# Attention and expert layers on one core: all expert matmuls as two halves side by side on 64x128 tiles

## The chip, the core and the metric

The kernel runs on one core of a Trainium2 chip. A core has five engines that run their own queues in order and meet at semaphores: TensorE (PE) for matmuls, VectorE (DVE), ScalarE (ACT), GpSimd (POOL) and SyncE (SP), which issues most DMAs. The metric is the device time of one execution in microseconds (us); lower is better.

## What is computed

Eight batches of 448 tokens, 12 heads of 64, all float32. First attention with capped scores, then a layer of one expert, in which each batch sends its 128 best tokens through two matrices:

```python
scores = cap * np.tanh(scale * np.matmul(q, k.transpose(0, 1, 3, 2)) / cap)
attn = np.exp(scores - max)
out = np.matmul(attn / (attn.sum(-1) + 1e-09), v)      # -> x, (8, 448, 768)
...
scores = np.einsum('bsd,d->bs', x, w_gate)
for b in range(B):
    top_idx = np.argpartition(-scores[b], capacity)[:capacity]   # 128 of 448
    xe = x[b, top_idx]
    ye = np.maximum(xe @ w1, 0.0) @ w2                  # 768 -> 1024 -> 768
    g = 1.0 / (1.0 + np.exp(-scores[b, top_idx]))
    out[b, top_idx] = x[b, top_idx] + g[:, None] * ye
```

## The kernel before

The order of all instructions on all engines is made before the program is built, by a planner inside the kernel (`Sim`, `Task`, `Front`): each step is a `Task` with an engine, an assumed duration, events that it depends on, and slots of rings (buffers) that it takes and releases. The planner plays the steps through and writes them out in that order; on the chip the engines keep this order and wait at semaphores. A wrong duration in it makes no error, only a wait.

**Attention** is done by a `Double`: four heads of one batch, 24 in all. A Double has four units of 128 keys, the last of 64; two such tails make one score unit, so there are 84 score units and 96 value units. A score unit (`scores_mm`) fills `K.S4`, four PSUM banks, of which there is one set. ACT turns it into one of four buffers `K.p` with a tanh, which frees `K.S4`, and an exponential in place (`score_task`). `values_mm` multiplies `p` with `v` (28 matmuls, each of two passes) and accumulates a Double's units in two PSUM banks, which DVE divides and evacuates (`output_proc`).

**Tile forms.** PE can split its 128 rows and columns. In the rows of the trace `64*128 64x448` means a part of 64 rows by 128 columns with a moving operand of 64 partitions by 448 elements. Scores of the first four Doubles and of all tails are float32 on 64x64 parts; the other scores are three products of split operands (`kh`, `kl`, `qh`, `ql`: a float32r part and the rest) on two 64x128 parts that work side by side, into different banks. Values use 128x64 parts (64x64 for tails). Everything of the expert uses the whole 128x128 array (`FULL`).

**The expert.** When a batch's three Doubles are out, `select_proc` sums the gate scores (`total`), joins the two halves of the last column with a matmul (`join`), turns the four columns into a row on all partitions with four transposes (`turn`), and copies the row out of PSUM. DVE compares every score with the row (`greater`, `ties`), which gives ranks, a one-hot matrix and, by `pick` on PE, the token numbers and scores. POOL gathers the rows of the 128 tokens from the output in DRAM. `expert_proc` transposes them (`split_tasks`), splits them into high and low, and multiplies by `w1` in two halves of 512 columns, 18 matmuls each; then relu, transposes, `w2` in two halves of 384 columns, 24 matmuls each; `combine` on DVE adds the result, and POOL scatters the rows back. Two PSUM banks (`T`, `H`) serve all of this until attention ends, when the six banks of scores and values are added.

**The order on PE** is chosen in `Front.policy` between the next score unit (Q), the next value unit (V) and expert steps (F). Costs of a change of form are `SWITCH` and `AFTER`; `LEAST`, `MOST` and `due` set how much expert work is put between, `second_value` lets a value unit wait for another. SP's queue holds the loads of q, k, v and the stores of the output, in the order planned.

Of the kernel before, what the change touches and what calls it, by code (L numbers as in the profile page):

```python
# [16 lines left out]
P = 128  # L17
HD = 64
# [6 lines left out]
FAR = 1e6  # L25


QUARTER, TALL, WIDTH, FULL = range(4)
SWITCH, AFTER = 100, 45
MARGIN = 150  # L30
RESERVE = 50000
LEAST, MOST = 1500, 2200
# [5 lines left out]
PS, PG, PH = 1.1, 1.1, 1.2  # L38
IDLE = 2000
# [181 lines left out]
def allocate(tc, K):  # L221
# [17 lines left out]
    K.twice = t("twice", [P, P])  # L239
# [3 lines left out]
    K.before = t("before", [P, NCH * P], BF16)  # L243
    K.gst = [t(f"gst{i}", [P, 4]) for i in range(2)]
    K.part = [t(f"part{i}", [P, K.NG, NCH]) for i in range(2)]
    K.jk, K.jt = t("jk", [P, S], BF16), t("jt", [P, S], BF16)
# [8 lines left out]
    K.p = ring("p", 4, [P, 4, S])  # L255
# [8 lines left out]
    K.row = ring("row", 1, [P, S])  # L264
# [15 lines left out]
    K.acc = [Ring([bank(tc, K.stack, f"V{i}", [P, 512])]) for i in range(2)]  # L280
    K.banks = Ring([bank(tc, K.stack, c, [P, 512]) for c in "TH"])


def lent(K, nm, dt):
    return K.work.tile([P, 2, K.S], dt, tag="x" + nm, name=nm + "lent")

# [11 lines left out]
def split_scores(tc, K):  # L298
    K.score_stack.close()
    K.score_stack = ExitStack()  # L300
    return [bank(tc, K.score_stack, c, [P, 512]) for c in "ABCD"]


def load_flag(tc, K, cap):
# [3 lines left out]
    warm = K.banks.slots[1].obj  # L308
# [9 lines left out]
def load_consts(tc, K):  # L318
# [75 lines left out]
class Double:  # L394

    def __init__(self, K, d):
# [5 lines left out]
        if d % 2:  # L402
            self.units = self.units[-1:] + self.units[:-1]
# [4 lines left out]
        self.accs = None  # L408
# [20 lines left out]
    def split(self, tc, K):  # L429
        nc = tc.nc  # L430
        for nm in "kq":
# [3 lines left out]
            def high(t, nm=nm, raw=raw):  # L435
# [7 lines left out]
                refs=[K.NCH - 1] * 2, prio=1.2, kind="high")  # L443
# [41 lines left out]
def values_mm(tc, K, D, c):  # L485
    p, v = D.P[c], D.at("v")
    full = K.NCH - 1
    for i in range(K.NS):
        for r in range(2):
            for g in range(2):  # L490
# [3 lines left out]
                tc.nc.tensor.matmul(D.accs[r].obj[HALF[g], i * WIDE:(i + 1) * WIDE],  # L494
# [15 lines left out]
def output_proc(tc, K, D):  # L510
# [9 lines left out]
    def evac(t, r):  # L520
# [3 lines left out]
        blocks = D.accs[r].obj[:, :K.NS * WIDE].rearrange("p (i w) -> p i w", w=WIDE)  # L524
# [51 lines left out]
def select_proc(tc, K, b):  # L576
# [5 lines left out]

    def total(t):
# [6 lines left out]
    t = yield Task("DVE", 380, total, deps=K.scored[b], take=[K.score], refs=[4 + 2 * NCH],  # L590
# [4 lines left out]
    last = NCH - 1  # L595

    def join(t):
        nc.tensor.matmul(t.slots[0].obj[:, S:S + 1], lhsT=K.twice, rhs=score[:, last:],
                         start=True, stop=True)
# [3 lines left out]
    bank, rs = j.slots  # L603
    row = rs.obj
    j = yield Task("DVE", 130, lambda t: nc.vector.tensor_copy(
        score[:, last:], bank.obj[:, S:S + 1]), deps=[j], reads=[sc], prio=1, kind="joined")

    def turn(t):
        for c in range(NCH):
            nc.tensor.transpose(bank.obj[:, c * P:(c + 1) * P],  # L610
                                score[:, c:c + 1].to_broadcast([P, P]), K.ident)
# [8 lines left out]
    for c in range(NCH):  # L620
# [5 lines left out]
        def ties(t, c=c):  # L626
            m = rows_of(c)
            n = min(P * (c + 1), S)
            at = P * (NCH - 1 - c)
            nc.vector.scalar_tensor_tensor(out=K.jt[:m, :n], in0=row[:m, :n],  # L630
                                           scalar=score[:m, c:c + 1],
                                           in1=K.before[:m, at:at + n],
# [16 lines left out]
    for n in range(chunks):  # L649
# [709 lines left out]
```

## Time and profile before

| | us |
|---|---|
| runs shown | 462.6, 464.11, 465.36 |
| median | 464.11 |
| profiled execution | 464.68 |
| its span, first to last instruction | 463.0 |
| PE busy | 446.5 |
| ACT busy | 311.1 |
| DVE busy | 264.6 |

The durations below come from the profiled execution. A row of the timeline has a start, the time to the end of the last of its instructions, and how many there are; matmuls overlap, so the step from one start to the next tells what one costs the queue. Floats of 32 bits that are no float32r run as two instructions each. In brackets stands an idle time ahead of the row and what released it. The mean clock granted to TensorE was 0.994 of full speed.

### The profile page before, as it was taken

What the parts mean: (1) busy time and instruction counts of PE and PEld (TensorE: products, weight loads), DVE (VectorE), ACT (ScalarE), POOL (GpSimd) and SP (SyncE); (2) the same over time, 40 slices, a digit from 0 to 9 for tenths busy, and PEclk for the clock granted to TensorE, in tenths of its full rate; (3) what the DMA queues carried; (4) which work ended last, traced back from release to release, by engine and by line L of the source; (5) the groups of instructions that cost most, each with busy time, mean ns of one, the idle gap of its engine ahead of it and who ended that gap; (6) DMA issues with size and microseconds to landing.
All of it is one profiled execution on the core that took longest, in us unless ns stands there. A gap on an engine that the chain in (4) does not pass through costs nothing.

```text
span 463.0 us, 16297 instructions
## 1 busy us (share of the span) xinstructions
PE 446.5 (96%) x7358; PEld 363.3 (78%) x7358; DVE 264.6 (57%) x784; ACT 311.1 (67%) x202; POOL 22.1 (5%) x53
## 2 busy tenths in 40 slices
PE   6999998999999999999999999999999998999994
PEld 3665676878878878788788788887787896988984
DVE  1087789977439735379368386674289336342321
ACT  4899999987886868795978896877869741010010
POOL 2000000100000001000001000001000001001000
PEclk9999999999999999999999999999999999999998
DMA  7977475355252253271272432434422102011001
GB/s 233 376 228 240 141 266 197 95 180 166 81 180 64 82 193 120 81 237 48 61 254 78 151 132 83 149 95 150 164 87 75 42 23 89 30 40 55 15 35 39
DMA packets 31886, 58.52 MB, mean 126 GB/s; under 512 B 9920, under 2 KB 19904, under 8 KB 31808
## 3 DMA queue, kind: packets, MB, share of 16 engines
q1 hardware_dynamic: 30528, 51.10, 34.0%
q0 software_dynamic: 1280, 6.29, 4.2%
q8 instruction: 59, 0.97, 0.9%
q14 instruction: 19, 0.16, 0.1%
HBM read 43.23 MB, written 14.16 MB: 124 GB/s over the span
## 4 chain that ended last, share of the span: by engine, by line
PE 79%; issue 10%; ACT 5%; DMA 3%; DVE 2%; SPq 0%; POOL 0%; POOLq 0%; DVEq 0%; ACTq 0%
PE psV L494 27%; PE psS L471 16%; PE psS L481 8%; PE psH L771 6%; PE psT L771 4%; PE psH L808 3%; ACT p L923 3%; PE psT L808 3%; PE psD L808 2%; PE psC L771 2%; PE psV L808 2%; ACT p L930 2%; DMA out<-xe,idx 2%; PE psT L710 1%; PE psA L808 1%
## 5 line engine op out<-in xcount | busy, mean ns | idle before, releaser
L923 ACT ACTIVATE p<-psS,sc 128x1792 f32<-128x1792 f32 x84 | 147.5, 1756 | 61.7 <-PE psS L471 42.9
L494 PEld LDWEIGHTS psV<-v,p 128*64 128x64 f32 (+1 forms) x5152 | 139.3, 137 | 24.9 <-issue 15.5
L930 ACT ACTIVATE p<-p,capc 128x1792 f32<-128x1792 f32 x84 | 150.6, 1792 | 2.4
L494 PE MATMUL psV<-v,p 128*64 128x65 f32 (+1 forms) x5152 | 148.6, 223 | 1.8 <-DVE xt L531 1.2
L471 PE MATMUL psS<-qh,kh 64*128 64x448 f32 x240 | 50.3, 415 | 1.3 <-ACT p L923 1.1
L481 PE MATMUL psS<-q,k 64*64 64x448 f32 x328 | 37.4, 572 | 3.7 <-ACT p L923 3.4
L440 DVE CAST kh<-k 128x896 fp32r<-128x896 f32 x20 | 12.5, 625 | 41.1 <-DMA k<-in_k 34.4
L525 DVE RECIPROCAL rec<-psV 128x7 f32<-128x7 f32 x48 | 9.6, 200 | 41.4 <-PE psV L494 41.4
L471 PEld LDWEIGHTS psS<-qh,kh 64*128 64x128 f32 x240 | 22.6, 184 | 12.2 <-issue 5.2
L560 DVE CUSTOM_DVE_ANT_0 jk<-xn,wg 128x256 bf16<-128x256 f32 x72 | 30.3, 420 | 1.2
L526 DVE TENSOR_TENSOR xn<-psV,rec 128x384 f32<-128x384 f32 x48 | 26.8, 558 | 1.7
L481 PEld LDWEIGHTS psS<-q,k 64*64 64x64 f32 x328 | 11.0, 137 | 16.8 <-issue 10.6
L471 PE MATMUL psS<-qh,kl 64*128 64x448 f32 x120 | 22.1, 362 | 0.0
L471 PE MATMUL psS<-ql,kh 64*128 64x448 f32 x120 | 22.1, 362 | 0.0
L471 PE MATMUL psS<-qh,klent 64*128 64x448 f32 x120 | 22.0, 363 | 0.0
L471 PE MATMUL psS<-qlent,kh 64*128 64x448 f32 x120 | 22.0, 362 | 0.0
L623 DVE TENSOR_SCALAR_CACHE_REDUCE jk<-row,score 128x448 bf16<-128x448 f32 (+1 forms) x32 | 21.5, 672 | 0.2
L784 ACT ACTIVATE hs<-psH 128x512 f32<-128x512 f32 x8 | 4.7, 593 | 24.4 <-PE psH L771 24.4
L683 ACT ACTIVATE gt<-gt 128x1 f32<-128x1 f32 x8 | 1.6, 194 | 26.0 <-DVE gt L680 25.9
L630 DVE SCALAR_TENSOR_TENSOR jt<-row,score,before 128x128 bf16<-128x128 f32 (+3 forms) x32 | 16.9, 527 | 0.0
L460 POOL MEMSET v<- 128x14 f32 x23 | 3.0, 132 | 265.7 <-DMA v<-in_v 196.6
L852 POOL DMA_INDIRECT out<-xe,idx x8 | 8.2, 1021 | 142.5 <-DVE xe L824 122.4
(212 smaller groups left out, 623.5 us busy)
## 6 DMA issues: line engine op xcount, KB each, us to landing
v<-in_v SPq DMA_DIRECT2D x23, 455.0 KB, 3.4
q<-in_q SPq DMA_DIRECT2D x22, 448.0 KB, 4.8
k<-in_k SPq DMA_DIRECT2D x22, 448.0 KB, 6.2
out<-xn SPq DMA_DIRECT2D x24, 384.0 KB, 2.9
stage<-in_moe_w SPq DMA_DIRECT2D x4, 512.0 KB, 7.3
stage<-in_moe_w SPq DMA_DIRECT2D x5, 384.0 KB, 4.3
out<-xt SPq DMA_DIRECT2D x48, 32.0 KB, 2.7
hs<-in_moe_w SPq DMA_DIRECT2D x3, 384.0 KB, 5.7
```

The source lines that it names most:

```text
L440: nc.vector.tensor_copy(t.slots[0].obj, self.at(nm))
L471: tc.nc.tensor.matmul(K.S4[:, 2 * r + j, :K.S], lhsT=a[HALF[j], r, c * P:(c + 1) * P], rhs=b[HALF[j], r, :], start=(n == 0), stop=(n == 2))
L481: tc.nc.tensor.matmul(K.S4[HALF[half], n, :K.S], lhsT=k[HALF[j], r, at:at + HD], rhs=q[HALF[j], r, :], start=True, stop=True)
L494: tc.nc.tensor.matmul(D.accs[r].obj[HALF[g], i * WIDE:(i + 1) * WIDE], lhsT=p[rows, h, n * HD:(n + 1) * HD], rhs=v[rows, u, :], start=(c = ...
L526: nc.vector.tensor_tensor(slots[0].obj.rearrange("p c (r j d) -> p r j c d", r=2, j=2)[:, r], blocks[:, :2 * full, :K.D].rearrange("p (j c ...
L560: nc.vector.tensor_tensor_reduce(out=K.jk[:, :x.shape[1]], in0=x, in1=g, scale=1.0, scalar=0.0, op0=ALU.mult, op1=ALU.add, accum_out=part[ ...
L623: nc.vector.tensor_scalar(K.jk[:m], row[:m], score[:m, c:c + 1], None, op0=ALU.is_gt, op1=ALU.add, accum_out=rk.obj[:m, 0, c:c + 1])
L630: nc.vector.scalar_tensor_tensor(out=K.jt[:m, :n], in0=row[:m, :n], scalar=score[:m, c:c + 1], in1=K.before[:m, at:at + n], op0=ALU.is_equ ...
L771: nc.tensor.matmul(ph[:M], lhsT=(xh, xl)[part][:, i, :M], rhs=K.wts[r][:, i, fs], start=(n == 0), stop=(n == len(ops) - 1))
L808: nc.tensor.matmul(bank[0].obj[:M, :HH], lhsT=hp[0].obj[part][:, i, :M], rhs=K.wts[r][:, i, ds_], start=(start and n == 0), stop=(stop and ...
L923: nc.scalar.activation(slot.obj, K.S4[:, :, :K.S], AF.Tanh, scale=K.sc)
L930: nc.scalar.activation(slot.obj, slot.obj, AF.Exp, scale=K.cap)
```

## The change

Every expert matmul (`group`) becomes two: the upper and lower 64 rows of the contraction, side by side on 64x128 parts. In the first turn of a layer rows 0 to 63 write the bank of the left half of the columns and rows 64 to 127 that of the right half; in the second turn they change banks. Between the turns stands a drain of PE. Transposes (`split_tasks`), which now do all of a layer's blocks into one slot, and `pick` are cut in the same way, and what reads them joins two banks. PSUM slots are pairs of banks: one slot `T` for the expert in place of `T` and `H`, one for the accumulators.

The row of scores no longer passes PE: `put` stores the 128x4 scores in a line in DRAM, `get` loads the line onto all partitions, and DVE joins the last column (`sums`). The row has the tokens in another order and is 512 long, so the masks for ties change.

In the planner `FULL` goes, `SWITCH` and `AFTER` are 110 and 85 for 100 and 45, expert steps may stand directly beside scores of their form, and value units come in runs of up to four or to the end of a Double (`run_ready`). From Double 6 on the tails' score unit stands ahead of the even Double instead of the odd one, and the even Double's values begin with the tail. Relu may run on DVE.

```diff
-SWITCH, AFTER = 100, 45
+SWITCH, AFTER = 110, 85
...
+LATE = 3000
+RUN, SLACK = 4, 300
+SIDE = 6
+DRAIN = 100
...
-        if d % 2:
+        if d % 2 == (1 if d < SIDE else 0):
             self.units = self.units[-1:] + self.units[:-1]
...
-    K.acc = [Ring([bank(tc, K.stack, f"V{i}", [P, 512])]) for i in range(2)]
-    K.banks = Ring([bank(tc, K.stack, c, [P, 512]) for c in "TH"])
+    K.acc = Ring([bank(tc, K.stack, "V", [P, 2, 512])])
+    K.banks = Ring([bank(tc, K.stack, "T", [P, 2, 512])])
...
-    j = yield Task("PE", 250, join, deps=[t], take=[K.banks, K.row], refs=[1, 2 * NCH],
-                   reads=[sc], prio=(0, 3 * b), kind="join")
...
-    r = yield Task("PE", 400, turn, deps=[j], reads=[sc], prio=(0, 3 * b), kind="turnrow")
-    r = yield copy_task(tc, S, lambda _: row, lambda _: bank.obj[:, :S], deps=[r],
-                        reads=[bank], prio=1, kind="rowcopy")
...
+    def put(t):
+        nc.sync.dma_start(t.slots[0].obj.rearrange("o (p c) -> (o p) c", c=NCH), score)
+
+    def get(t):
+        nc.sync.dma_start(t.slots[0].obj, ln.obj.to_broadcast([P, NCH * P]))
+
+    def sums(t):
+        tail = places[:, :HD, last]
+        nc.vector.tensor_tensor(tail, tail, places[:, HD:, last], op=ALU.add)
+        nc.vector.memset(places[:, HD:, last], NEVER)
+        nc.vector.tensor_tensor_reduce(out=K.jk[:HD, :HD], in0=tail[:HD], in1=K.ident[:HD, :HD],
+                                       scale=1.0, scalar=0.0, op0=ALU.mult, op1=ALU.add,
+                                       accum_out=score[:HD, last:])
+
+    w = yield Task("SP", 700, put, deps=[t], take=[K.line], refs=[1], reads=[sc], lag=900, prio=0,
+                   kind="put")
+    ln = w.slots[0]
+    r = yield Task("SP", 700, get, deps=[w], take=[K.row], refs=[2 * NCH], reads=[ln], lag=900,
+                   prio=0, kind="get")
...
+    r = yield Task("DVE", 600, sums, deps=[(r, LATE)], reads=[sc], prio=1, kind="joined")
...
-                nc.tensor.matmul(t.slots[0].obj[:, :4], lhsT=sel.obj[:, c, :],
-                                 rhs=vals[:, :, c], start=(c == 0), stop=(c == NCH - 1))
+                for h, half in enumerate(HALF):
+                    nc.tensor.matmul(t.slots[0].obj[:, h, :4], lhsT=sel.obj[half, c, :],
+                                     rhs=vals[half, :, c], start=(c == 0), stop=(c == NCH - 1))
...
         for i in range(w):
-            nc.tensor.transpose(pt[:, i, :M], src[:M, (at + i) * P:(at + i + 1) * P],
-                                K.ident[:M, :M])
+            for h, half in enumerate(HALF):
+                nc.tensor.transpose(t.slots[0].obj[:, h, i * HD:(i + 1) * HD],
+                                    src()[half, i * P:(i + 1) * P], K.ident[half, half])
...
+def group(tc, K, kind, prio, pair, parts, wts, n, width, cost):
+    nc = tc.nc
+    ops = [(0, wts + "h", i) for i in range(n)] + [(0, wts + "l", i) for i in range(n)]
+    ops += [(1, wts + "h", i) for i in range(n)]
+    last = len(ops) - 1
...
+    for m in range(2 * len(ops)):
+        turn, at = divmod(m, len(ops))
+        part, r, i = ops[at]
...
+            if m == last + 1:
+                gap.append(nc.tensor.drain().ins)
...
+            for h in (0, 1) if m != last else (1, 0):
+                g = h ^ turn
+                ins = nc.tensor.matmul(bank.obj[:, g, :width],
+                                       lhsT=pair.obj[part][HALF[h], i, :],
+                                       rhs=K.wts[r][HALF[h], i, g * width:(g + 1) * width],
+                                       start=(m == 0), stop=(m == 2 * last + 1)).ins
...
+            if D.d >= SIDE and D.d % 2 == 0:
+                self.work.append([(D, full), (Ds[D.d + 1], full)])
...
-        if seg == "F":
-            order = "FQV" if self.left > 0 else "QVF"
-        elif f and not big and not self.backlog(t, IDLE):
-            order = "VFQ" if seg == "Q" and two else "FVQ" if seg == "Q" else "QFV"
...
+        run = self.run_ready(t)
+        if run:
             order = "VQF"
...
+            order = "QFV"
```

The order of instructions shows it in two places. First PE, where the first layer of the second batch's expert is multiplied. L471 is a score unit (six such rows make one), L771 an expert matmul into bank `psT` or `psH`, L494 values. Before, from a score unit on:

```order
L471 MATMUL psS<-qh_104,klent 128x448 x2
L771 MATMUL psT<-w1l,xh 128x512 x5
L771 MATMUL psT<-w1h,xl 128x512 x5
L471 MATMUL psS<-qh_103,kh_101 128x448 x2
...
L471 MATMUL psS<-qh_103,kl_105 128x448 x2
L494 MATMUL psV_129<-v_88,p_90 64x65 x2
...
L494 MATMUL psV_133<-v_88,p_91 64x65 x2
...
L771 MATMUL psT<-w1h,xl 128x512
L771 MATMUL psH<-w1h,xh 128x512 x6
```

After, the same layer (L484 scores, L778 expert halves, two to a pair, L507 values, 28 to a unit):

```order
L484 MATMUL psS<-qh_104,kl_106 128x448 x2
L778 MATMUL psT<-w1h,xh 128x512 x12
L778 MATMUL psT<-w1l,xh 128x512 x6
L484 MATMUL psS<-qh_104,kh_102 128x448 x2
...
L778 MATMUL psT<-w1h,xh 128x512 x10
L778 MATMUL psT<-w1l,xh 128x512 x10
L507 MATMUL psV<-v_90,plent 64x65 x28
L507 MATMUL psV<-v_90,p_91 64x65 x28
L507 MATMUL psV<-v_90,p_92 64x65 x28
L507 MATMUL psV<-v_90,p_93 64x65 x28
```

Scores and expert halves alternate in three score units, and four value units follow in one run, where two stood between two score units.

Second SP, at a batch's last output stores in the middle of the program (`xn`, `xt` are stored, `v`, `q`, `k` loaded). Before:

```order
L546 DMA out<-xn_95 384x1x256
L549 DMA out<-xt_98 64x2x64 x2
L415 DMA q_85<-in_q 128x896
L415 DMA k_87<-in_k 128x896
L415 DMA q_84<-in_q 128x896
```

After:

```order
L559 DMA out<-xn_95 384x1x256
L562 DMA out<-xt_99 64x2x64 x2
L611 DMA line_113<-score_116 128x4
L614 DMA row_110<-line_113 128x512
L428 DMA v_89<-in_v 128x910
```

The store of the scores and the load of the row stand between the output's stores and the next loads.

## Rows read from the trace of the kernel before

**Rows 1.** The page: PE's line of part 1, and part 4 by engine.
```profile
PE 446.5 (96%) x7358; PEld 363.3 (78%) x7358; DVE 264.6 (57%) x784; ACT 311.1 (67%) x202; POOL 22.1 (5%) x53
PE 79%; issue 10%; ACT 5%; DMA 3%; DVE 2%; SPq 0%; POOL 0%; POOLq 0%; DVEq 0%; ACTq 0%
```
**Rows 2.** Busy time of each engine in four stretches.
```profile
0.00:95.00 95.00, 86.93 (x1774) 61.62 (x1776) 64.78 (x175) 81.98 (x49) 4.46 (x22) 0.98 0.68 224
95.00:378.00 283.00, 282.48 (x5171) 232.62 (x5169) 168.69 (x526) 221.99 (x140) 9.81 (x23) 1.00 0.37 118
378.00:457.20 79.20, 77.05 (x425) 69.02 (x421) 30.94 (x84) 7.15 (x14) 6.84 (x7) 1.00 0.13 42
457.20:463.00 5.80, 0.00 (x0) 0.00 (x0) 0.23 (x1) 0.00 (x0) 0.97 (x1) 0.79 0.21 75
```
**Rows 3.** Timeline of PE: start us, us, instruction; scores, expert, scores.
```profile
177.21 0.48 PE L471 MATMUL psS<-qh,kh 64*128 64x448 f32 x2
177.52 0.37 PE L471 MATMUL psS<-qlent,kh 64*128 64x448 f32 x2
...
178.34 0.37 PE L471 MATMUL psS<-qh,klent 64*128 64x448 f32 x2
178.63 1.43 PE L771 MATMUL psT<-w1l,xh 128*128 128x512 f32 x5
...
181.16 0.47 PE L471 MATMUL psS<-qh,kh 64*128 64x448 f32 x2
```
**Rows 4.** Timeline of PE: one value unit, three in a row, one tail.
```profile
223.28 1.85 PE L494 MATMUL psV<-v,p 128*64 128x65 f32 x56
225.06 0.47 PE L471 MATMUL psS<-qh,kh 64*128 64x448 f32 x2
...
276.20 5.12 PE L494 MATMUL psV<-v,p 128*64 128x65 f32 x168
281.25 0.47 PE L471 MATMUL psS<-qh,kh 64*128 64x448 f32 x2
...
235.08 1.05 PE L494 MATMUL psV<-v,p 64*64 64x65 f32 x56
236.05 0.79 PE L808 MATMUL psT<-w2h,hh 128*128 128x384 f32 x3
```
**Rows 5.** Timeline of PE: expert matmuls undisturbed, w1 and w2.
```profile
438.99 1.56 PE L771 MATMUL psH<-w1h,xh 128*128 128x512 f32 x6
440.39 1.56 PE L771 MATMUL psH<-w1l,xh 128*128 128x512 f32 x6
...
453.14 0.86 PE L808 MATMUL psT<-w2l,hh 128*128 128x384 f32 x4
453.83 0.85 PE L808 MATMUL psT<-w2h,hl 128*128 128x384 f32 x4
```
**Rows 6.** Timeline of PE: joining and turning the row, and transposes of the expert.
```profile
383.26 0.36 PE L598 MATMUL psB<-score,twice 128*128 128x1 f32 x2
383.48 0.48 PE L771 MATMUL psH<-w1l,xh 128*128 128x512 f32 x1
...
386.13 0.65 PE L610 MATMUL psB<-ident,score 128*128 128x128 f32 x4 [1.70 <-DVE score L605]
386.54 0.72 PE L771 MATMUL psH<-w1h,xl 128*128 128x512 f32 x2
...
407.45 0.60 PE L710 MATMUL psV<-ident,hs 128*128 128x128 f32 x4
407.81 0.48 PE L771 MATMUL psC<-w1h,xh 128*128 128x512 f32 x1
408.12 1.10 PE L771 MATMUL psC<-w1l,xh 128*128 128x512 f32 x4
```
**Rows 7.** Timeline of PE's weight loads in a score unit.
```profile
177.52 0.19 PEld L471 LDWEIGHTS psS<-qh,klent 64*128 64x128 f32 x2
177.73 0.19 PEld L471 LDWEIGHTS psS<-qh,kh 64*128 64x128 f32 x2
```
**Rows 8.** Timeline of ACT, where it is never idle.
```profile
88.59 1.73 ACT L923 ACTIVATE p<-psS,sc 128x1792 f32<-128x1792 f32 x1
90.35 1.79 ACT L930 ACTIVATE p<-p,capc 128x1792 f32<-128x1792 f32 x1
...
95.80 1.76 ACT L923 ACTIVATE p<-psS,sc 128x1792 f32<-128x1792 f32 x1
```
**Rows 9.** DMA issues (KB each, us to landing), and what SP's queue waited for.
```profile
k<-in_k SPq DMA_DIRECT2D x22, 448.0 KB, 6.2
out<-xt SPq DMA_DIRECT2D x48, 32.0 KB, 2.7
xe<-out,idx POOLq DMA_INDIRECT x8, 3.9
SPq L415 <- PE psV L494: 132.9, 24, 10.8
```
**Rows 10.** Timeline from attention's end to the last batch's pick: PE, DVE, PE.
```profile
378.31 0.79 PE L808 MATMUL psT<-w2h,hh 128*128 128x384 f32 x3
...
382.41 0.16 DVE L587 TENSOR_TENSOR score<-score,part 128x4 f32<-128x4 f32 x1
385.59 0.16 DVE L678 TENSOR_SCALAR idx<-psA 128x1 int32<-128x1 f32 x1 [3.02 <-DMA out<-xe,idx]
...
386.82 0.62 DVE L505 COPY row<-psB 128x448 f32<-128x448 f32 x1 [0.19 <-PE psB L610]
...
394.19 0.86 DVE L661 TENSOR_SCALAR sel<-iota,rk 128x128 fp32r<-128x128 f32 x4
...
403.98 0.50 PE L670 MATMUL psD<-vals,sel 128*128 128x4 f32 x4
```
**Rows 11.** Timeline of the end.
```profile
456.81 0.62 DVE L824 SCALAR_TENSOR_TENSOR xe<-psA,gt,xe 128x384 f32<-128x384 f32 x1 [1.47 <-PE psA L808]
```

More of the change, by code (lines that the diff above doesn't have):

```diff
@@ L263, in allocate @@
         raw.free.append(raw.slots[-1])
-    K.row = ring("row", 1, [P, S])
+    K.row = ring("row", 1, [P, NCH * P])
+    lines = K.stack.enter_context(tc.tile_pool(name="lines", bufs=1, space=bass.MemoryType.DRAM))
+    K.line = Ring([lines.tile([1, NCH * P], F32, name=f"line{i}") for i in range(2)])
     K.sel = ring("sel", 1, [P, NCH, P], F32R)
@@ L581, in select_proc @@
     part = K.part[b % 2]
+    last = NCH - 1
     def total(t):
@@ L589, in select_proc @@
     chunks = -(-K.C // P)
-    t = yield Task("DVE", 380, total, deps=K.scored[b], take=[K.score], refs=[4 + 2 * NCH],
+    t = yield Task("DVE", 380, total, deps=K.scored[b], take=[K.score], refs=[3 + 2 * NCH],
                    prio=1, kind="total")
@@ L593, in select_proc @@
     score = sc.obj
[L595 to L599, printed above, removed]
-    j = yield Task("PE", 250, join, deps=[t], take=[K.banks, K.row], refs=[1, 2 * NCH],
-                   reads=[sc], prio=(0, 3 * b), kind="join")
-    bank, rs = j.slots
-    row = rs.obj
[L605 to L611, printed above, removed]
-    r = yield Task("PE", 400, turn, deps=[j], reads=[sc], prio=(0, 3 * b), kind="turnrow")
-    r = yield copy_task(tc, S, lambda _: row, lambda _: bank.obj[:, :S], deps=[r],
-                        reads=[bank], prio=1, kind="rowcopy")
+    def put(t):
[14 more added lines that the diff above has]
+                   prio=0, kind="get")
+    rs = r.slots[0]
+    row = rs.obj
+    places = row.rearrange("p (a c) -> p a c", c=NCH)
+    r = yield Task("DVE", 600, sums, deps=[(r, LATE)], reads=[sc], prio=1, kind="joined")
     r = [r]
@@ new lines, in turn @@
+            for h, half in enumerate(HALF):
+                nc.tensor.transpose(t.slots[0].obj[:, h, i * HD:(i + 1) * HD],
+                                    src()[half, i * P:(i + 1) * P], K.ident[half, half])
+    t = yield Task("PE", 111 * w, turn, deps=dep, take=[K.banks, take],
+                   refs=[2 * len(parts), 0], reads=reads, prio=prio, kind=kind)
+    bank, pair = t.slots
+    if take is K.xs and not isinstance(pair.obj, tuple):
+        pair.obj = (K.work.tile([P, K.ND, P], F32R, tag="xh", name="xh"), K.xl)
@@ new lines, in expert_proc @@
+    yield [t]
+    hp, parts = yield from split_tasks(tc, K, lambda: relus[0].obj, [t], K.hp, [relus[0]],
+                                       K.NF, (0, 3 * b + 2), "turnh")
+    hp.refs = 1
+    yield [K.weights["w2"]]
+    if not K.tail:
+        yield [p for pair in parts.values() for p in pair]
+    HH = K.DM // 2
+    bank, t = yield from group(tc, K, "w2", prio, hp, parts, "w2", K.NF, HH, 177)
+    ends = [sim.add(Task("DVE", 534, lambda _, g=g: nc.vector.scalar_tensor_tensor(
+        out=xe.obj[:, g * HH:(g + 1) * HH], in0=bank.obj[:, g, :HH], scalar=gt.obj,
+        in1=xe.obj[:, g * HH:(g + 1) * HH], op0=ALU.mult, op1=ALU.add), deps=[t, gate],
+        reads=[bank, gt], prio=1, kind="combine")) for g in range(2)]
```

366 lines of the change are left out of this document (150 added, 216 removed).

## The prediction

> **What bounds the kernel now.** I read the page first. TensorE (PE) is busy 446.5 of 463.0 us and the chain that ended last lies on it for 79% [rows 1]. The table of stretches says where the rest is: up to 95 us PE is busy 86.93 us and ScalarE (ACT) 81.98; from 95 to 378 us, while scores, values and expert work alternate, PE is busy 282.48 of 283.00; from there to 457.2 us it works off the experts that are left, 77.05 of 79.20; the last 5.8 us are the end of the last expert [rows 2]. So from 95 us on the time is what stands in PE's queue, laid end to end. "Busy" hides gaps in a pipelined engine, so I went to start times. A score unit on 64x128 tiles starts at 177.21, its pairs of matmuls follow each other every 0.205 us (177.52 to 178.34, four steps), and the expert's first matmul starts at 178.63: 1.42 us for six pairs that need 6 x 0.205 = 1.23 [rows 3]. The ten expert matmuls behind it take 178.63 to 181.16 = 2.53 us; where such matmuls run undisturbed six take 1.40 us (0.233 each), so ten need 2.33 [rows 3, 5]. Values on 128x64 tiles: one block of 28 takes 1.78 us, three in a row 5.05, so a block needs 1.635 and a run pays 0.145 once; on 64x64 tiles a block takes 0.97 [rows 4]. **Each run of one tile form thus pays about 0.19 (scores), 0.20 (expert), 0.15 us (values)**, half behind its last matmul and half before its second.
>
> **Runs of one form.** Counting runs in the two instruction orders gives 202 before (60 of 64x128, 53 of 128x64, 48 of 128x128, 41 of 64x64) and 133 after (45, 51, 1, 36): the expert's runs join those of the scores. 15 x 0.19 + 47 x 0.20 + 2 x 0.145 + 5 x 0.15 = **-13.3 us**.
>
> **The score row leaves PE.** Per batch the joining matmul (383.26 to 383.48, 0.22) and the four turning transposes (386.13 to 386.54, 0.41) go: 8 x 0.63 = **-5.1 us**; the wait of 1.70 us for the joined column, once, goes too, **-1.7** [rows 6].
>
> **Expert matmuls.** 672 whole ones become 672 pairs of halves. A score pair, two halves side by side, takes 0.205 us for 448 columns; whole matmuls take 0.233 for 512 and 0.69/4 = 0.173 for 384 [rows 3, 5], and between these 448 would be 0.203. So a pair costs a whole one: 0. The 112 transposes become pairs of half the width. Now one takes (0.67 - 0.233)/4 = 0.11 us [rows 6]. A pair may take half of that (-6 us in all), if only columns count, or twice (+12), if the two weight loads came one after the other. But a score pair's two loads end together, 0.19 us for both [rows 7], so I take 0 again, and likewise for the 32 picks.
>
> **Drains.** Each of 16 layers is cut once by a drain, where the halves change banks. The trace has no such instruction. The nearest row is a change of form, 0.20 us [rows 3]; less than nothing it can't be, since the queue only waits there; twice that is my upper end. 16 x 0.20 = **+3.2** (0 to 6.4).
>
> **ACT.** A unit occupies ACT for a tanh and an exponential, 88.59 to 95.80 us for two units, 3.6 us each where ACT is the limit [rows 8]. Where PE comes to the next scores sooner, it waits. I added up what stands in PE's order between one score unit and the next. Past the 24th unit, where expert work begins, six such periods in the old order are under 3.55 us and lack 1.4 us of 3.6 in all. In the new one there are 22, lacking 5.6, for two reasons: a run without changes is shorter for the same work (score, 18 halves: 1.23 + 2.10 plus one change), and with one PSUM slot for all expert steps there is none to lay between while a layer is emptied. **+4.2** (0, if the slack after long value runs absorbs it, to 7, if ACT's copies of 0.5 us fall there). The first 24 units stay ACT's: nothing gained there.
>
> **The row through DRAM.** SP gets a store and a broadcast load per batch; the load waits for the store's landing, and loads of v, q, k queue behind it. They have cover: SP already spends 132.9 us in 24 waits for PE to release v [rows 9]. The chain from total to pick grows. A landing takes 2.7 us (small store) to 6.2 (k) [rows 9], so two take 5.4 to 12.4. For the last batch the total is ready at 382.6, 4.3 us after attention's end (378.31), and from the row's copy at 386.82 to the one-hot at 394.19 to 395.05 are 8.2 us; its pick ran only at 403.98 [rows 10]. After the change some 22 us of PE work (expert matmuls and transposes, by the steps above) stand between the last values and that pick. The chain needs 4.3 + 5.4 to 12.4 + about 9 = 19 to 26 us. VectorE (DVE) also waited 3.02 us for an earlier scatter to release the index [rows 10], and the transposes of the next tokens follow the pick by about 5 us of PE work, where a gather takes 3.9 to land [rows 9]. In the tail I put **+1.5** (0 to 4). Elsewhere the experts run a batch behind the attention, and wider comparisons (512 for 448) lie on a DVE that is busy 168.69 of 283 us [rows 2].
>
> **The end.** The two halves of the last layer finish together, so a second combine of 0.62 us [rows 11] follows the first: **+0.6**. The scatter after it is the same.
>
> **Sum.** -13.3 - 5.1 - 1.7 + 3.2 + 4.2 + 1.5 + 0.6 = -10.6 us. The profiled execution took 464.68 us (span 463.0), inside the 462.6 to 465.36 of the runs with median 464.11; 464.68 - 10.6 = 454.1, against the median 453.5. I say **454.0 us**. All favourable ends give 464.68 - 20.1 + 0.6 - 6 = 439; all adverse ends without the transposes' give 464.68 - 20.1 + 6.4 + 7 + 4 + 0.6 = 462.6. Both need everything to fall one way.
>
> **Rivals.**
> 1. *The cost sits in the hand-over, not in the form.* If a run of scores followed by expert work pays the half behind its last matmul (0.1 us) though the form stays, 77 such hand-overs in the new order cost 7.7 us: **461.7**. Against it: four transposes and an expert matmul, different operands and banks of one form, take 0.67 us, against 0.41 for four turning transposes and 0.233 [rows 5, 6]: 0.03 over. For it: no row has a score next to an expert matmul in the same form.
> 2. *Each further matmul costs (slower than before).* The new order has 816 more matmuls (672, 112, 32). If each took 13 ns beyond its share of a pair, the 10.6 us are gone; from there on the kernel is slower. The row that shows something beyond columns is the transpose: 0.11 us [rows 6], where 128 columns by the slope of the expert matmuls, (0.233 - 0.173)/128 each [rows 5], are 0.06. At half of these 50 ns, 25 ns for each of 816, it takes 454.1 + 20.4 = **474.5**. Against it: score pairs, two instructions per 0.205 us, lie on the line of the whole matmuls [rows 3, 5]. For it: the narrowest pairs (384, 64 and 4 columns) have no row in this form. The Trainium skill, "TensorEngine Tiling (Array Packing)", section Instruction Overhead, speaks for this one: each matmul has about 60 cycles of overhead, however narrow. At 2.4 GHz that is 25 ns, an estimate from that page, and 474.5 as well; by that rule, side by side halves would not be free, and the score pairs disagree.
> 3. *The row comes late.* DVE takes its queue in order. If the landing comes after the time that the planner assumed, DVE stands at the first sum, evacuations and splits behind it wait, and PE behind them. Eight batches at 1 us: **462**; from 1.3 us each the gain is gone.
> 4. *Nothing is lost to drains and ACT.* 454.1 - 3.2 - 4.2 = **446.7**.
>
> **How the numbers follow.** Forecast (448 to 460) 0.70; rival 1 0.08, rival 2 0.06, rival 3 0.08, rival 4 0.08. A measurement tells apart about 0.5%, 2.3 us: faster is below 461.8, slower above 466.4. Faster gets the forecast, rival 4 and about half of rivals 1 and 3, less some for what I did not see: 0.82. Same, the other half of 1 and some of 3: 0.09. Slower, rival 2 and the bad end of 3: 0.09. The range runs from 448, a little above rival 4, to 462, with rival 1 in it and rival 2 left out.
>
> **What would show it.** Right: from 95 us on no bare 128x128 run; a score unit 1.23 us up to an expert pair behind it; expert pairs every 0.23 and 0.17 us; each drain's gap near 0.2 us; the last values ending near 386 us, for more expert work done by then, and a tail of some 60 us in place of 79. Wrong: pairs slower than that (rival 2), a gap of 0.1 us between score and expert matmul (rival 1), PE waits whose releaser is a DVE instruction that itself waited for the row (rival 3), PE waits for tanh over 7 us past 95 us.

## The result, and the profile after

The changed kernel takes 457.73 us (median of 4 runs, 454.75 to 458.72) against 464.74 us before: a ratio of 0.9847, 95% interval 0.9813 to 0.9881. A control in a later comparison (c_after, below) gave 0.9870 (0.9829 to 0.9910). Where an experiment is set against the changed kernel I take the mean of both, 0.9859, and 1% as 4.65 us. 454.0 was predicted, with a range of 448 to 462.

The profiled execution took 458.26 us, its span is 456.5 (463.0 before). The page's line of PE and its chain by engine:

```profile
PE 431.3 (94%) x8126; PEld 360.5 (79%) x8126; DVE 276.1 (60%) x847; ACT 303.0 (66%) x191; POOL 23.6 (5%) x55
PE 80%; ACT 7%; DMA 5%; issue 3%; DVE 3%; SPq 1%; POOL 0%; DVEq 0%; POOLq 0%; ACTq 0%
```

PE is busy 15.2 us less than in [rows 1], but the span fell by 6.5 only: PE stands more. The table of stretches, cut at the same events as [rows 2] (per stretch: us, then busy us of PE, weight loads, DVE, ACT, POOL, the granted clock, DMA share, GB/s):

```profile
0.00:95.00 95.00, 84.39 (x1776) 58.95 (x1778) 62.17 (x170) 81.19 (x49) 5.09 (x23) 0.98 0.71 235
95.00:388.80 293.80, 287.40 (x5726) 249.35 (x5724) 186.55 (x592) 217.90 (x135) 12.93 (x27) 0.99 0.37 120
388.80:449.60 60.80, 59.53 (x634) 52.21 (x626) 26.24 (x84) 3.91 (x8) 4.59 (x5) 1.00 0.15 47
449.60:456.50 6.90, 0.00 (x0) 0.00 (x0) 1.14 (x2) 0.00 (x0) 0.96 (x1) 0.84 0.17 63
```

Attention ends 10.5 us later, with more expert work done by then, and the tail is 60.8 us in place of 79.2. From 95 us to attention's end PE now stands 6.4 us, where it stood 0.5; 1.0 of it are ten drains, with an idle of 0.1 us each. Next a score unit between expert pairs, from PE's timeline (start us, length, instruction), the counterpart of [rows 3]:

```profile
160.35 0.86 PE L778 MATMUL psT<-w1l,xh 64*128 64x512 f32 x6
161.05 0.39 PE L484 MATMUL psS<-qh,kh 64*128 64x448 f32 x2
161.28 0.37 PE L484 MATMUL psS<-ql,kh 64*128 64x448 f32 x2
...
162.09 0.37 PE L484 MATMUL psS<-qh,kl 64*128 64x448 f32 x2
162.30 0.86 PE L778 MATMUL psT<-w1l,xh 64*128 64x512 f32 x6
163.00 0.86 PE L778 MATMUL psT<-w1h,xl 64*128 64x512 f32 x6
```

The unit takes 161.05 to 162.30 = 1.25 us, against 6 x 0.205 = 1.23: nothing is paid at either hand-over. It isn't one case: from 95 us on 19 score units stand between expert matmuls without a wait, median 1.25 us (1.22 to 1.34); 27 with values ahead of them and expert steps behind, where one change of form remains, have a median of 1.32. Three expert pairs take 162.30 to 163.00 = 0.70, so 0.233 each, as the whole matmuls of [rows 5]. A layer's first half and its drain, in the tail:

```profile
395.37 1.56 PE L778 MATMUL psA<-w1h,xl 64*128 64x512 f32 x12
397.04 1.67 PE L778 MATMUL psA<-w1h,xh 64*128 64x512 f32 x12
398.53 1.58 PE L778 MATMUL psA<-w1l,xh 64*128 64x512 f32 x12
399.93 1.57 PE L778 MATMUL psA<-w1h,xl 64*128 64x512 f32 x12
```

Six pairs need 1.40 us (398.53 to 399.93). The step that ends in the drain takes 1.67, the one behind it 1.49: the drain costs 0.27 before and 0.09 behind it, 0.36 in all.

What PE waited for between 95 us and attention's end (us in total, times, longest):

```profile
PE psS L484 <- ACT p L911: 1.5, 2, 1.2
PE psV L507 <- issue: 1.3, 1, 1.3
PE psV L507 <- DVE both L697: 1.0, 1, 1.0
PE psV L507 <- ACT p L918: 0.6, 1, 0.6
PE psT L732 <- issue: 0.5, 1, 0.5
PE psT L778 <- DVE xl L748: 0.4, 1, 0.4
```

The two longest follow each other, where no expert work was at hand:

```profile
357.39 0.71 PE L732 MATMUL psT<-ident,hs 64*128 64x64 f32 x16
359.33 0.47 PE L484 MATMUL psS<-qh,kh 64*128 64x448 f32 x2 [1.23 <-ACT p L911]
...
362.11 1.80 PE L507 MATMUL psV<-v,p 64*64 64x65 f32 x56 [1.29 <-issue]
363.84 0.90 PE L732 MATMUL psT<-ident,xe 64*128 64x64 f32 x12
```

The 56 value matmuls here take 1.73 us, against 0.97 in [rows 4]. The stretches say why (the clock is the third number from the end):

```profile
355.00:359.00 4.00, 3.10 (x88) 1.81 (x88) 3.47 (x11) 1.47 (x1) 0.00 (x0) 1.00 0.39 119
359.00:362.00 3.00, 1.49 (x12) 1.05 (x12) 2.96 (x12) 2.54 (x4) 0.13 (x1) 1.00 0.50 155
362.00:365.50 3.50, 3.39 (x74) 3.22 (x76) 2.31 (x11) 3.45 (x3) 0.00 (x0) 0.51 0.02 5
```

PE was busy 4.59 of 7.0 us, and then ran at a granted clock of 0.51, the lower of its two levels (1.2 GHz). With 3.39 us busy at half speed this costs 1.7 us, a cost that the prediction does not have.

### The profile page after: what moved, and what is told of

Read it like the earlier page. It is cut to its first block, busy times and chain, and to the rows that moved or that the text cites. A ratio compares the mean times of both kernels' runs of the same rounds, so it can differ in the third digit from the quotient of the medians.

```text
span 456.5 us, 17936 instructions
## 1 busy us (share of the span) xinstructions
PE 431.3 (94%) x8126; PEld 360.5 (79%) x8126; DVE 276.1 (60%) x847; ACT 303.0 (66%) x191; POOL 23.6 (5%) x55
## 4 chain that ended last, share of the span: by engine, by line
PE 80%; ACT 7%; DMA 5%; issue 3%; DVE 3%; SPq 1%; POOL 0%; DVEq 0%; POOLq 0%; ACTq 0%
PE psV L507 27%; PE psT L778 22%; PE psS L484 16%; PE psS L494 7%; ACT p L911 4%; PE psA L778 4%; ACT p L918 2%; PE psB L778 2%; DMA row<-line 1%; PE psT L732 1%; DMA xe<-out,idx 1%; DMA k<-in_k 1%; ACT plent L911 1%; DMA out<-p,idx 1%; DMA q<-in_q 1%
## 5 line engine op out<-in xcount | busy, mean ns | idle before, releaser
L911 ACT ACTIVATE p<-psS,sc 128x1792 f32<-128x1792 f32 x63 | 110.3, 1750 | 63.8 <-PE psS L494 34.2
L507 PEld LDWEIGHTS psV<-v,p 128*64 128x64 f32 (+1 forms) x3864 | 106.0, 139 | 23.4 <-issue 11.6
L507 PE MATMUL psV<-v,p 128*64 128x65 f32 (+1 forms) x3864 | 113.5, 225 | 5.9 <-issue 2.0
L918 ACT ACTIVATE p<-p,capc 128x1792 f32<-128x1792 f32 x63 | 112.9, 1793 | 1.7
L484 PE MATMUL psS<-qh,kh 64*128 64x448 f32 x240 | 49.1, 405 | 2.3 <-ACT p L911 2.1
L911 ACT ACTIVATE plent<-psS,sc 128x1792 f32<-128x1792 f32 x21 | 36.8, 1752 | 14.4 <-PE psS L484 7.7
L494 PE MATMUL psS<-q,k 64*64 64x448 f32 x328 | 37.3, 569 | 3.9 <-ACT p L911 2.7
L918 ACT ACTIVATE plent<-plent,capc 128x1792 f32<-128x1792 f32 x21 | 37.6, 1793 | 0.7
L507 PEld LDWEIGHTS psV<-v,plent 128*64 128x64 f32 (+1 forms) x1288 | 34.8, 137 | 4.1 <-issue 2.7
L507 PE MATMUL psV<-v,plent 128*64 128x65 f32 (+1 forms) x1288 | 37.7, 223 | 0.3 <-issue 0.2
L484 PEld LDWEIGHTS psS<-qh,kh 64*128 64x128 f32 x240 | 22.8, 185 | 9.0 <-ACT p L911 4.5
L640 DVE TENSOR_SCALAR_CACHE_REDUCE jk<-row,score 128x512 bf16<-128x512 f32 (+1 forms) x32 | 23.7, 740 | 0.8
L494 PEld LDWEIGHTS psS<-q,k 64*64 64x64 f32 x328 | 11.8, 138 | 15.6 <-issue 9.0
L484 PE MATMUL psS<-ql,kh 64*128 64x448 f32 x120 | 22.3, 366 | 0.0
L778 PE MATMUL psT<-w2h,hh 64*128 64x384 f32 x192 | 21.3, 345 | 1.0 <-DVE xl L748 0.4
L484 PE MATMUL psS<-qh,kl 64*128 64x448 f32 x120 | 22.1, 363 | 0.0
L484 PE MATMUL psS<-qlent,kh 64*128 64x448 f32 x120 | 21.9, 362 | 0.0
L484 PE MATMUL psS<-qh,klent 64*128 64x448 f32 x120 | 21.9, 362 | 0.0
```

Source lines behind the costliest of these rows:

```text
L484: tc.nc.tensor.matmul(K.S4[:, 2 * r + j, :K.S], lhsT=a[HALF[j], r, c * P:(c + 1) * P], rhs=b[HALF[j], r, :], start=(n == 0), stop=(n == 2))
L494: tc.nc.tensor.matmul(K.S4[HALF[half], n, :K.S], lhsT=k[HALF[j], r, at:at + HD], rhs=q[HALF[j], r, :], start=True, stop=True)
L507: tc.nc.tensor.matmul(D.acc.obj[HALF[g], r, i * WIDE:(i + 1) * WIDE], lhsT=p[rows, h, n * HD:(n + 1) * HD], rhs=v[rows, u, :], start=(c == ...
L640: nc.vector.tensor_scalar(K.jk[:m], row[:m], score[:m, c:c + 1], None, op0=ALU.is_gt, op1=ALU.add, accum_out=rk.obj[:m, 0, c:c + 1])
L778: ins = nc.tensor.matmul(bank.obj[:, g, :width], lhsT=pair.obj[part][HALF[h], i, :], rhs=K.wts[r][HALF[h], i, g * width:(g + 1) * width], ...
L911: nc.scalar.activation(slot.obj, K.S4[:, :, :K.S], AF.Tanh, scale=K.sc)
```

## The experiments

To compare traces I split PE's time from its first to its last matmul. *Work* is the number of instructions times the step at which they follow each other undisturbed (score pair 0.205, value pair 0.058 or 0.029 us, expert 0.233 and 0.173, transpose 0.103 whole or 0.058 as a pair). *Waits* is the idle time that the profile puts ahead of PE's instructions; the idle of 0.1 us at each drain is in it, 1.6 us in the changed kernel and 7.5 in e3_drains. *Rest* is what is left: changes of form, drains, stretches at the lower clock.

| kernel | ratio to before (95%) | runs of one form | drains | work | waits | rest |
|---|---|---|---|---|---|---|
| before | 1 | 202 | 0 | 404.0 | 10.3 | 40.9 |
| changed | 0.9847 (0.9813–0.9881) | 133 | 16 | 394.0 | 18.3 | 35.7 |
| c_after | 0.9870 (0.9829–0.9910) | 133 | 16 | 394.0 | 19.1 | 33.5 |
| e4_rowdram | 0.9943 (0.9918–0.9968) | 206 | 0 | 398.9 | 11.8 | 44.1 |
| e1_whole | 1.0088 (1.0057–1.0118) | 206 | 0 | 398.9 | 18.7 | 43.2 |
| e10_oldrules | 1.0109 (1.0076–1.0143) | 173 | 16 | 394.0 | 23.3 | 43.6 |
| e10_oldrules6 | 0.9982 (0.9955–1.0010) | 150 | 16 | 394.0 | 24.0 | 38.7 |
| e5_run1 | 1.0194 (1.0151–1.0238) | 185 | 16 | 394.0 | 26.4 | 42.5 |
| e2_turn2 | 0.9943 (0.9914–0.9972) | 133 | 16 | 400.5 | 18.4 | 34.2 |
| e3_drains | 1.0354 (1.0315–1.0393) | 133 | 80 | 394.0 | 25.6 | 52.7 |
| e7_noexp | 0.9767 (0.9730–0.9804) | 133 | 16 | 394.0 | 17.6 | 33.3 |
| e8_noexp_b | 1.0004 (0.9974–1.0033) | 202 | 0 | 404.0 | 10.6 | 41.8 |
| e9_slack0 | 0.9776 (0.9737–0.9816) | 133 | 16 | 394.0 | 17.4 | 33.8 |
| e9_late1 | 0.9827 (0.9785–0.9869) | 127 | 16 | 394.0 | 18.1 | 34.1 |

With 1.7 us taken off for each stretch at the lower clock (those at the start, near 10 us, included), a straight line through the rest of 13 of these 14 profiles gives 0.18 us for a run of one form and 0.27 for a drain, and misses none by more than 1.1 us. With a drain's idle of 0.1 us, which stands under waits, that is the 0.36 of the steps above. The one left out, e10_oldrules6, had four such stretches and lies 3 us below the line.

**e1_whole: the halves undone.**

```diff
-            for h in (0, 1) if m != last else (1, 0):
-                g = h ^ turn
-                ins = nc.tensor.matmul(bank.obj[:, g, :width],
-                                       lhsT=pair.obj[part][HALF[h], i, :],
...
+            nc.tensor.matmul(bank.obj[:, turn, :width], lhsT=pair.obj[part][:, i, :],
+                             rhs=K.wts[r][:, i, turn * width:(turn + 1) * width],
+                             start=(at == 0), stop=(at == last))
```

> The expert's matmuls, transposes and picks on whole 128x128 tiles again, without drains; the planner's rules and the row through DRAM as in the changed kernel. By the instruction order 206 runs of one tile form in place of 133. Theory (the halves gain because a run of one form costs, 0.13 to 0.19 us each): +73 runs = +9.5 to +13.9, 16 drains gone = -4.0, transposes whole again = +5.5, and up to 4 us of waits for ScalarE fewer: 7 to 15 us above the changed kernel, so 0 to 8 us above the kernel before. Rival (the gain is the row's and the planner's, the halves bring nothing): only drains and transposes, 1.5 us above the changed kernel, some 5.5 below the kernel before.

Measured: 10.6 us above the changed kernel, 4.1 above the one before. The theory holds. By the split: work +4.9, rest +7.5, waits +0.4. Under the changed planner's rules the halves are worth more than the whole gain.

**e4_rowdram: the row's way alone, on the kernel before.**

```diff
-    j = yield Task("PE", 250, join, deps=[t], take=[K.banks, K.row], refs=[1, 2 * NCH],
...
-    r = yield Task("PE", 400, turn, deps=[j], reads=[sc], prio=(0, 3 * b), kind="turnrow")
...
+    w = yield Task("SP", 700, put, deps=[t], take=[K.line], refs=[1], reads=[sc], lag=900, prio=0,
...
+    r = yield Task("SP", 700, get, deps=[w], take=[K.row], refs=[2 * NCH], reads=[ln], lag=900,
...
```

> The kernel before with one part of the change alone: the score row goes through a line in DRAM, with the wider comparisons on VectorE; the expert stays on 128x128 tiles, the planner's rules are the old ones. Theory (as in the prediction): eight joins and turns leave TensorE, seven of them where it sets the time, 7 x 0.63 = -4.4, the wait of 1.70 us goes, +0 to +4 for a later row in the tail: 2 to 6 us below the kernel before. Rival (VectorE stands at the late row, evacuations and splits behind it wait, TensorE behind them): 0 to 8 us above it.

Measured: 2.7 us below the kernel before, at the theory's lower end. The rival's first half is true: DVE stood 12.3 us at the row. But PE waits only 1.5 us more in all. Work fell by 5.1; the rest is 3.2 us larger, with four runs more and one more stretch at the lower clock (at 68.8 us). From what DVE waited for, in this kernel, in the changed one and in e9_late1:

```profile
DVE row L606 <- DMA row<-line: 12.3, 3, 5.8
DVE row L618 <- DMA row<-line: 1.6, 1, 1.6
DVE row L618 <- DMA row<-line: 5.0, 4, 1.7
```

**e10_oldrules: the halves and the row under the old rules, and e10_oldrules6.**

```diff
-SWITCH, AFTER = 110, 85
+SWITCH, AFTER = 100, 45
...
-MOST = 4000
+LEAST, MOST = 1500, 2200
...
-RUN, SLACK = 4, 300
-
-SIDE = 6
+SIDE = 24
+IDLE = 2000
...
-        run = self.run_ready(t)
+        if seg == "F":
+            order = "FQV" if self.left > 0 else "QVF"
...
```

e10_oldrules6 is the same with SIDE = 6.

> The changed kernel (halves, drains, row through DRAM) with the rules, costs and order of the tail units of the planner before: what the halves bring without the longer runs of values. By the instruction order 173 runs of one tile form, against 206 with the same rules and whole matmuls (run e4_rowdram). Theory (terms as now measured: 0.156 us a run, 0.35 a drain, transposes -5.5): -33 x 0.156 = -5.1, +5.6, -5.5 = -5.0 against e4_rowdram, 0 to 4 back in waits for ScalarE: 459 to 463 us where the kernel before takes 466. Rival (halves bring their 12 us, as between e1_whole and the changed kernel, under any rules): 452.

> As e10_oldrules, but the tail units of two neighbouring head groups stand in the order of the changed kernel. By the instruction order 150 runs of one tile form. Theory (runs are what counts): 23 runs fewer, -3.6 us against e10_oldrules, give or take 2 us for waits. Rival (the rules for values decide, not the tail units): within 1 us of e10_oldrules.

Measured: e10_oldrules 11.6 us above the changed kernel and 5.1 above the one before, which neither theory nor rival allows. Against e4_rowdram it gained 4.9 us of work, as reckoned, but its waits rose from 11.8 to 23.3, by 9.3 of these 11.5 us past 95 us (1.6 of it at drains). From the waits there:

```profile
PE psV L506 <- ACT plent L918: 1.4, 1, 1.4
...
PE psT L777 <- DVE xe L831: 1.2, 1, 1.2
PE psS L483 <- ACT p L911: 1.1, 3, 0.5
PE psT L686 <- DVE xl L747: 0.9, 1, 0.9
```

Values wait for exponentials, and expert steps for the one PSUM slot that DVE must empty (`xe`, `xl`); no single cause. DVE stood longer at the late row (rival 3) here than in any other kernel:

```profile
DVE row L617 <- DMA row<-line: 22.4, 4, 6.1
```

In e10_oldrules6 DVE has no such wait, and yet PE waits as long, 24.0 us against 23.3, which speaks against the row as the main cause. Four kernels now make a square, in us against the kernel before:

| | old rules | new rules |
|---|---|---|
| whole matmuls, row through DRAM | -2.7 (e4_rowdram) | +4.1 (e1_whole) |
| halves, row through DRAM | +5.1 (e10_oldrules) | -6.6 (changed) |

Two sides of the square change one thing: under the new rules the halves gain 10.6 us, and with halves the new rules gain 11.6. The other two start from e4_rowdram, which alone keeps the old PSUM slots (`T` and `H` apart, one per accumulator) and transposes a layer in parts. So the 7.7 us lost by the halves under the old rules, and the 6.7 us lost by the new rules with whole matmuls, hold this layout as well; no run parts the two. Halves, layout and rules together gain 3.9 on top of the row. e10_oldrules6 has 23 runs fewer than e10_oldrules and comes out 5.9 us below it, where 3.6 give or take 2 was expected: the order of the tail units alone is half of what the new rules give.

**e5_run1: shorter runs of values.** `RUN, SLACK = 4, 300` becomes `RUN, SLACK = 1, 300`.

> The changed kernel with a planner that turns to values as soon as one unit of them is ready, not four: 189 runs of one tile form in place of 133. Theory (each run costs 0.13 to 0.19 us): +7 to +11, less what more mixed work hides of the 6.4 us in which TensorE waits between 95 us and the end of attention: +1 to +11 above the changed kernel, +6 in the middle. Rival (runs of one form cost next to nothing, it is the waits that decide): 3 to 6 us below the changed kernel.

Measured: +15.6, above both. The 52 runs more (185 by the profile) cost about what they should, 52 x 0.18 = 9.4: the rest rose by 6.8, or by 10.2 without the two stretches at the lower clock that only the changed kernel's profile has. But waits rose by 8.1 instead of falling. Past 95 us:

```profile
PE psV L507 <- DVE xt L544: 4.0, 13, 0.3
...
PE psT L732 <- DMA xe<-out,idx: 1.8, 2, 1.2
PE psV L732 <- DMA p<-out,idx: 1.1, 1, 1.1
```

Values come up to VectorE's emptying of their PSUM bank, 13 times; attention ends at 337 us, and in the longer tail the gathers are no longer covered.

**e3_drains: more drains.**

```diff
+            if at in (n, 2 * n):
+                nc.tensor.drain()
             for h in (0, 1) if m != last else (1, 0):
```

> The changed kernel, with two more drains in the first half of each of the 16 layers, at places where no row changes its bank: 32 more drains. Theory (the step across a drain is 0.25 us longer than a step without one because the drain empties the queue): +8.0 us, 6 to 8 if some of it falls into waits. Rival (the 0.25 us is the price of the halves that change banks behind it, a drain by itself is nearly free): 0 to +1.

The condition holds in both halves of a layer, so 64 drains were added, not 32. Measured: +23.0 us, 23.0 / 64 = 0.36 each, where the theory had 0.25. Starts in the tail, a drain ahead of each of the three rows:

```profile
411.95 1.67 PE L780 MATMUL psA<-w1h,xl 64*128 64x512 f32 x12
413.73 1.66 PE L780 MATMUL psA<-w1h,xh 64*128 64x512 f32 x12
415.50 1.67 PE L780 MATMUL psA<-w1l,xh 64*128 64x512 f32 x12
```

1.77 to 1.78 for six pairs that need 1.40. The rival falls: a drain costs this where nothing changes banks.

**e2_turn2: each pair of transposes twice.** The two `nc.tensor.transpose` of a pair are issued a second time.

> The changed kernel, with each of the expert's 112 pairs of half transposes issued twice in a row, with the same result. Theory (a pair costs the 0.0575 us by which the starts of the pairs follow each other, half of a whole transpose's 0.11): +6.4 us, a little less where TensorE waits anyway: 5 to 6.4 above the changed kernel. Rival (a pair costs what a whole one cost, as the prediction took it): +12.3.

Measured: +3.9 us, a little under the theory (the interval of its ratio alone is 1.3 us to either side; the profiled spans, 461.5 and 456.5, differ by 5.0). The rival falls. Starts of single pairs, issued at L732 and again at L735:

```profile
405.05 0.22 PE L732 MATMUL psB<-ident,p 64*128 64x64 f32 x2
405.10 0.23 PE L735 MATMUL psB<-ident,p 64*128 64x64 f32 x2
405.17 0.23 PE L732 MATMUL psB<-ident,p 64*128 64x64 f32 x2
```

0.06 us a pair, half of a whole one's 0.11 [rows 6].

**e7_noexp and e8_noexp_b: ScalarE relieved.** In the changed kernel, and in the one before:

```diff
-                nc.scalar.activation(slot.obj, slot.obj, AF.Exp, scale=K.cap)
+                part = slot.obj[:, :1, :8] if u >= 24 else slot.obj
+                nc.scalar.activation(part, part, AF.Exp, scale=K.cap)
```

> The changed kernel in the same order of instructions, but from the 25th score unit on ScalarE's exponential takes only 8 columns of one row block (the values then use the tanh: this part of the computation is left out). Theory (TensorE waits for ScalarE, which gets shorter periods between scores): of the 6.4 us in which TensorE stands between 95 us and the end of attention most go, 4 to 6, and 1.7 us more with the stretch of 3.4 us at the lower clock that followed the two longest waits: 5 to 8 us below the changed kernel. Rival (these waits are VectorE's or a DMA's): 0 to 1.5 us below it.

> The same on the kernel before: from the 25th score unit on the exponential takes only 8 columns of one row block (left out of the computation as well). Theory: the old order leaves ScalarE more time between scores, TensorE stands 0.5 us for it between 95 us and the end of attention: 0 to 1.5 us below the kernel before. Rival (ScalarE holds both kernels alike): 4 us or more below it.

Measured: 4.3 us below the changed kernel, between theory and rival; no change (1.0004) in the kernel before, as expected. The waits past 95 us that are left in e7_noexp:

```profile
PE psS L484 <- ACT p L911: 1.7, 3, 1.2
PE psV L507 <- DVE both L697: 1.0, 1, 1.0
PE psV L507 <- issue: 0.7, 2, 0.5
```

The waits of values for an exponential are gone (0.6 at L918, and the 1.29 at 362 us). The 1.23 of the score unit stays although ScalarE has half its work: it waits for the tanh of the unit before (L911), which must first empty the only PSUM tile of scores. That is a chain of score, tanh and score with nothing laid between, not a ScalarE without time.

**e9_slack0, e9_late1 and the control.** `SLACK` 300 becomes 0; in e9_late1, `LATE` 3000 becomes 1000; c_after is the changed kernel.

> The changed kernel with the planner's allowance of 300 ns gone by which a value unit may be late when a run of values is begun: the order is the same up to about 350 us, then scores, transposes and values stand otherwise in it, so that the two waits of 1.23 and 1.29 us at 359 and 362 us should not arise. Theory (these waits cost what they show, and the 3.4 us at the lower clock behind them another 1.7): 2 to 4 us below the changed kernel, no stretch at the lower clock there. Rival (the waits only move elsewhere): within 1 us of the changed kernel.

> The changed kernel with the planner reckoning the row's landing 2 us earlier (1000 ns behind its usual time for a load in place of 3000): expert work starts earlier, 127 runs of one form in place of 133, and in the order no stretch of scores, transposes and values without expert matmuls near 360 us. Theory (no pair of waits there, no lower clock behind it, 6 runs fewer): 2 to 5 us below the changed kernel. Rival (the 3000 ns are needed: VectorE stands at the row in each batch, evacuations and splits behind it): 0 to 5 us above it.

> The changed kernel itself once more, as a control: the comparisons with it rest on four executions of it, whose mean clock was 0.984 to 0.996. Theory (the 3.3 us between it and e9_slack0 are the waits near 360 us and the stretch at the lower clock): its ratio to the kernel before stays at 0.983 to 0.987, 0.6% or more above the 0.9776 of e9_slack0, and a stretch at the lower clock behind 360 us is there again where the profile has one outside the first 16 us. Rival (the four executions were a poor sample): ratio 0.978 to 0.981, no difference to e9_slack0 that can be told.

Measured: e9_slack0 3.9 us below the changed kernel, e9_late1 1.5 (too close to tell), the control where the theory put it. c_after shows the same waits, 1.23 us at 357.96 and 1.29 at 360.74, and the same fall of the clock behind them; in e9_slack0 PE is busy and the clock stays up. c_after, then e9_slack0:

```profile
357.60:360.70 3.10, 1.49 (x12) 1.05 (x12) 3.07 (x13) 2.64 (x4) 0.12 (x1) 0.99 0.49 155
360.70:364.10 3.40, 3.36 (x74) 3.19 (x76) 2.21 (x11) 3.37 (x2) 0.00 (x0) 0.51 0.02 5
...
355.00:359.00 4.00, 4.00 (x48) 2.30 (x42) 3.56 (x13) 2.23 (x2) 0.00 (x0) 1.00 0.45 156
359.00:362.00 3.00, 2.61 (x84) 2.14 (x80) 2.96 (x8) 2.97 (x3) 0.12 (x1) 1.00 0.36 106
```

So the wait pair is 1.8 us (2.52 against 0.73 left) of the 3.9. The rest isn't settled, nor is the clock's part in it: e9_slack0's profile has a stretch at the lower clock elsewhere, behind 128 us, which the changed kernel's has not. e9_slack0 is the fastest full version of the study, 455.24 us against 466.23 of the kernel before in its comparison; its interval (0.9737 to 0.9816) only touches that of the changed kernel.

## Why the prediction was right, and where its terms were off

The sum was -10.6 us; the two profiles differ by 6.5, the medians by 7.0. Step by step:

| step of the prediction | predicted | in the profile |
|---|---|---|
| score row's matmuls leave PE | -5.1 | -5.0 |
| 112 transposes become pairs | 0 | -5.0 |
| 69 runs of one form fewer | -13.3 | -11.1 |
| 16 drains | +3.2 | +5.8 |
| waits without the drains' idle: join -1.7, ACT +4.2, tail +1.5 | +4.0 | +6.4 |
| lower clock at 362 us | – | +1.7 |
| the end | +0.6 | +0.7 |
| sum | -10.6 | -6.5 |

The rows of work and of drains are counts times the steps read from starts, and the row of runs is what is left, so it carries their errors.

- **Work.** 404.0 to 394.0, half of it the row's, half the transposes'. The prediction bounded the pairs from -6 to +12 and took 0; the lower bound, "if only columns count", was all but right. (For the row 8 x 0.63 is 5.04, where the sum has 5.1.)
- **Drains.** It took the price of a change of form, 0.20. Steps and e3_drains give 0.36: 16 x 0.36 = 5.8, inside its 0 to 6.4.
- **Runs of one form.** The rest fell by 5.2. Of the drains' 5.8 us 4.2 lie in it and 1.6 in the waits; with these 4.2 and 1.7 for the clock, 11.1 were saved, 0.16 a run, where 0.15 to 0.20 was read from rows (0.19 on average). The line through 13 profiles gives 0.18, and the kernel before lies 1.1 us below it. This was the step on which the forecast stood, and it held, at five sixths of its size.
- **Waits.** Up to 95 us they rose by 2.5, unforeseen ("nothing gained there" was all it said). From there to attention's end they rose by 5.9, of which 1.0 is the drains' idle: 4.9 in place of 4.2. In the tail the join's 1.70 is gone; new are 0.65 for `hs` and 0.6 at drains, and nothing for the late row, where 1.5 was put. The size was near, the reason half wrong: it counted ScalarE's 3.6 us a unit, but e7_noexp leaves the 1.23 us wait standing. Only some 1.9 us were for exponentials, and 1.9 more were for VectorE and for an issue, which the sum did not have.
- **Luck.** Runs (2.2), drains (2.6), waits (2.4) and the clock (1.7) all came out dearer than the sum had them, some 9 us together; the transposes gave 5.0 back that it did not have. Without that the time would have been some 463 us, past the end of the range. The mechanism held; that the figure came within 4 us is in part luck.
- **Rival 1** (hand-over in one form) falls by the score units between expert pairs, 1.25 us in the median of 19.
- **Rival 2** (each further matmul costs) falls by the pairs, 0.233 us. The Trainium skill, "TensorEngine Tiling (Array Packing)", section Instruction Overhead, would put about 25 ns (an estimate from its 60 cycles) on each of 816; no row here shows them, and transposes as pairs even halved.
- **Rival 3** (the row late) is real on DVE where the plan reckons differently, 12.3 us in e4_rowdram and 22.4 in e10_oldrules; in the changed kernel DVE stood 1.6 us once. PE waited 1.5 us more in e4_rowdram, and in e10_oldrules no less than in e10_oldrules6, where DVE doesn't stand at the row.
- **Rival 4** (nothing lost) falls by drains and waits.

Of what would show it, the last values end at 388.8 (386 predicted), the tail is 60.8 (60), and past 95 us PE waits 1.5 us for a tanh (L911), under the 7 that would have been a sign of error. A drain's gap near 0.2 us did not come; it is 0.27 ahead and 0.36 in all.

What the prediction did not see: that the halves need the new rules. It priced the parts as if they added up; e10_oldrules shows the same halves, with the PSUM layout that they bring, losing 7.7 us. The changed order had all its terms read from the order itself, so the sum came out, but as a claim on halves alone it would have been wrong.

## What to carry to other kernels

When most of an engine's time is laid end to end, count changes of tile form and price one from starts in the trace; here 0.18 us each, with the drains and the stretches at the lower clock, explained the rest of 13 kernels within 1.1 us. Price a drain apart: 0.36 us, twice a change of form. Then look for the place where the filling work runs out: closing one such place, by one constant of the planner, gave 3.9 us more, over half of what the large change gave; 1.8 of it are waits seen to go, the cause of the others is open.

## What the runs showed of the hardware that I had not expected

- Two 64-row transposes side by side, 64 columns each, follow each other every 0.06 us; a whole one needs 0.11.
- A drain costs 0.36 us (0.27 ahead of the next pair, 0.09 behind it) with nothing else to wait for.
- PE's clock fell to its lower level in the middle of the program, in the changed kernel after 7.0 us in which PE was busy 4.59, in the control after the same waits. It is not certain each time: e2_turn2 has 3.27 and 2.71 of 4.00 us busy from 360 to 368 us and keeps the clock there.
- Executions of one kernel differ with their mean granted clock: the changed kernel took 454.75 us at 0.996, 457.19 at 0.991, 458.26 at 0.990 and 458.72 at 0.984.
